# Program order on the DMA queue, later input requests, longer runs for v, and scaling ahead of the exponentials in a fused retention and mixture-of-attention kernel

## The chip, the cores and the metric

The kernel runs on one core of one Trainium2 chip. The metric is the device time of one execution in microseconds (us); lower is better. Engines are named as in the profile: PE is TensorE (PEld its weight loads), DVE is VectorE, ACT is ScalarE, POOL is GpSimd, SP is SyncE, which here only issues DMAs.

## The reference, cut to what matters

Eight batches, sequence S = 576. First a causal retention with decay over eight heads of width 64; its result x (576 x 512 per batch) goes into a second stage, a causal softmax attention for four experts, whose outputs are mixed with the weights of the two best experts of each token.

```
scores = (q @ k.T) / 8                       # per head, 576 x 576
x      = (scores * gamma**(i-j) * causal) @ v
logits = x @ w_gate;  w = softmax over the top 2 of 4 experts
for e in range(4):
    qe, ke, ve = x @ wq[e], x @ wk[e], x @ wv[e]
    a  = softmax(causal(qe @ ke.T / 8))
    out += w[e] * (a @ ve) @ wo[e]           # only where e is among the top 2
```

All is float32; the projections, v and the output product are done with operands split into a high and a low part (three products each).

## The kernel before, in words

**Tiles.** A batch is five chunks of tokens: four of 128 and one of 64 (CH, L20). The main loop (L532) runs n over 40 chunks of all batches and two more; in step n the retention works on chunk n and n-1, and the softmax attention on chunk n-6 (LAG, L26). Step n belongs to one of five kinds, n mod 5, because the heavier work of the second stage is dealt out by a table (STEPS, L448 to L461):

- kind 3: projections to q and k for tokens 0 to 255 (kq0);
- kind 4: projection to v for those tokens (v0, two tiles) and two output blocks (o0);
- kind 0: the two other output blocks of o0 and four of o1 (tokens 256 to 575), six in all;
- kind 1: half of the projections kq1 for tokens 256 to 575, and v1 (three tiles);
- kind 2: the other half of kq1, with the product of attention weights and v (`values`, L408) dealt between its pieces.

**One step** (L532 to L581) issues, in this order: `load(n + 2)` (two input DMAs, x and vk); `factors` (L374: three small DVE operations that make the row factors of the chunk whose exponentials ran one step earlier); `qk` (L127), the first part of `result` (L146: products `old` and `own`, ACT copies `old` out of PSUM at L168, DVE adds at L183), `state` (L106, product `st`); `scores(n - 6)` (L323: product `ss`; DVE masks each row block and takes its maximum, L361 or L365, tile nm; ACT takes the exponential in place with the row sum, L369); gate work; the rest of `result` (POOL multiplies at L188, and scales the next vk by L104; ACT rounds to xh at L191; POOL makes xl at L193); then the work of the table. Between the pieces of that work it deals `spread` (L402): one `scale` (L385: ACT multiplies a block of the exponentials by its row factor, L389) followed by one `turn` (L392: DVE transposes the block into TA and TB, L397 and L399). In a step of kind 2 the scales are dealt between the pieces, and the turns come after all of them, because `values` still reads TA and TB.

**PSUM** has eight banks, one pool (L42, L50). A product's bank comes free when ACT or DVE has copied it out: `pj` of a projection at L240 and L242, `pv` at L263, `po` of an output block at L442 (ACT) or L440 (DVE), `ys` of values at L424 and L425. The tile ot behind an output block has four buffers (L438), each free again when its output DMA (L443) has landed.

**v by way of HBM.** v is projected with tokens on partitions and needed in another arrangement, so it is written to HBM (tile hv, L267 and L268, one DMA) and read back with four DMAs (`back`, L274 to L279), one for each quarter of the partitions of vq. The runs that these four read are 512 bytes (128 floats). `back` is called behind the whole work of the step after the one that wrote hv (L574 to L578). vq for tokens 256 to 575 has one buffer, so its read waits until `values` of the batch before has read the old one.

**Order.** PE, DVE, ACT and POOL keep the order of the program (ORDERED, L15, `manual_schedule` at L43). SP isn't among them: the order of its DMAs is the compiler's, from its own planned times, and each waits in the queue for the one ahead.

**The tail** (L489) does the last five chunks of the last batch, with no retention beside it.

The functions that the diff touches, and what calls them:

Of the kernel before, what the change touches and what calls it, by code (L numbers as in the profile page):

```python
# [8 lines left out]
F32 = mybir.dt.float32  # L9
# [2 lines left out]
AF = mybir.ActivationFunctionType  # L12
OP = mybir.AluOpType
AX = mybir.AxisListType
ORDERED = {mybir.EngineType.PE, mybir.EngineType.DVE, mybir.EngineType.Activation, mybir.EngineType.Pool}  # L15

B, H, S, D = 8, 8, 576, 64
E, DM = 4, 512
# [5 lines left out]
NC = 5 * B  # L24

LAG = 6  # L26
# [7 lines left out]
def kernel(ctx: ExitStack, tc: tile.TileContext, xf, xt, vkf, vkt,  # L34
                                                    wraw, gi_d, con_d, out):
    nc = tc.nc
# [4 lines left out]
    hbm = ctx.enter_context(tc.tile_pool(name="hbm", bufs=2, space=bass.MemoryType.DRAM))  # L41
# [7 lines left out]
    def bank(shape, name):  # L49
        return pool.tile(shape, F32, name=name, tag="b")  # L50
# [31 lines left out]
    QUAD = [slice(32 * g, 32 * g + 32) for g in range(4)]  # L82
# [115 lines left out]
    W, QK, VN, WT = {}, {}, {}, {}  # L198
# [46 lines left out]
    def vproj(b, r, t):  # L245
        r0, n, tiles = RNG[r]
        nt = len(tiles)
        t0, C = CH[t]
        l0, ti = t0 - r0, t - tiles[0]
        xh, xl = XR[b, r]  # L250
        if ti == 0:
            VN[b, r] = (sb.tile([128, nt, NWV], F32, name=f"vn{r}", bufs=1),
                        sb.tile([128, 4 * nt, 2 * D], F32, name=f"vq{r}", bufs=2 - r))
        vn, vq = VN[b, r]
        ps = bank([128, NWV], "pv")
        i = 0
        for xx, ww in ((xh, W["v"][0]), (xh, W["v"][1]), (xl, W["v"][0])):
            for kc in range(4):
                mm(ps, xx[:, kc, l0:l0 + 128], ww[:, kc], start=(i == 0), stop=(i == 11))  # L259
                i += 1  # L260
                if i % 4 == 0 and i < 12:
                    yield
        act(vn[:, ti], ps, AF.Copy)  # L263
        if t == tiles[-1]:
            GATES.append(gate(b, r))

            hv = hbm.tile([128 * nt, E * D], F32, name=f"hv{r}")  # L267
            nc.sync.dma_start(hv.rearrange("(t p) c -> p t c", p=128), vn[:, :, :E * D])  # L268
            LATER.append((vq, hv))
        yield  # L270

    LATER = []

    def back():  # L274
        while LATER:
            vq, hv = LATER.pop()
            for g in range(4):
                p = g // 2
                nc.sync.dma_start(vq[QUAD[g]], hv[:, 128 * p:128 * p + 128].rearrange("(j r) c -> r j c", r=32))  # L279


    GATES = []
# [91 lines left out]
    def factors(m):  # L374
        b, t = divmod(m, 5)
        r = 0 if t < 2 else 1
        ti = t - RNG[r][2][0]
        p32, sm, ws = SS[m]
        n = len(ws)
        rs = sm[:, 1, :n]  # L380
        v.tensor_scalar(sm[:, 0, :n], sm[:, 0, :n], 1e-9, None, op0=OP.add)
        v.reciprocal(rs, sm[:, 0, :n])
        v.tensor_mul(rs, rs, WT[b, r][:, ti].rearrange("p i z -> p (i z)")[:, :n])  # L383

    def scale(m):  # L385
        p32, sm, ws = SS[m]
        for u, w in enumerate(ws):
            x = p32[:, u, :w]
            act(x, x, AF.Copy, scale=sm[:, 1, u:u + 1])  # L389
            yield  # L390

    def turn(m):  # L392
        p32, sm, ws = SS.pop(m)
        for u, w in enumerate(ws):
            z, k, nb = u % 2, 2 * (m % 5) + u // 2, w // 32
            x = p32[:, u, :w].rearrange("p (j c) -> p j c", c=32)
            v.transpose(TA[:, :min(nb, 8), z, k], x[:, :min(nb, 8)])  # L397
            if nb > 8:
                v.transpose(TB[:, :nb - 8, z, k - 4], x[:, 8:])  # L399
            yield  # L400

    def spread(m):  # L402
        a, b = scale(m), turn(m)
        for _ in a:
            next(b)
            yield

    def values(b, s0, s1):  # L408
        py = [bank([128, s1 - s0, 32], "ys") for g in range(4)]
        for j in range(2 * s1):  # L410
            sj = max(s0, j // 2)
            vq, jj = VN[b, 0 if j < 8 else 1][1], j % 8 if j < 8 else j - 8
            for z in range(2):
                tt = TA[:, j, z, sj:s1] if j < 8 else TB[:, j - 8, z, sj - 4:s1 - 4]
                for g in range(4):
                    mm(py[g][HALF[z], sj - s0:], vq[QUAD[g], jj, D * z:D * z + D], tt[QUAD[g]],  # L416
                       start=(j == 0), stop=(j == 2 * s1 - 1))
            if j % 6 == 5 and j < 2 * s1 - 1:
                yield
        if b not in YU:  # L420
            YU[b] = [sb.tile([128, 2, 9, 2, 32], F32R, name=x, bufs=1) for x in ("yh", "yl")]
        for g in range(4):
            hi, lo = (y[:, g // 2, s0:s1, g % 2] for y in YU[b])
            act(hi, py[g], AF.Copy)  # L424
            v.tensor_sub(lo, py[g], f(hi))  # L425
        yield
# [21 lines left out]
    STEPS = {}  # L448
# [14 lines left out]
    def work(n):  # L463
        vals = [values(b, 0, 9) for b, kind, part in STEPS.get(n, []) if kind == "y"]
        for b, kind, part in STEPS.get(n, []):
            if kind == "y":
                continue
            r, i = int(kind[-1]), 0
            if kind[:-1] == "kq":
                for p in range(2) if part is None else [part]:  # L470
                    for w in "kq":
                        for _ in proj(b, r, w, p):
                            i += 1
                            for y in vals[:i % 2 == 0]:
                                next(y, None)
                            yield
            elif kind[:-1] == "v":
                for t in RNG[r][2] if part is None else [part]:
                    yield from vproj(b, r, t)
            else:  # L480
                for d in part:
                    yield from outproj(b, r, d)

    def run(g):
        for _ in g:
            pass


    def tail():  # L489
        b = B - 1  # L490
        t0 = NC - 5

        def beside(g, *hs):
            for _ in g:
                for h in hs:
                    next(h, None)

        def outs(b, r):
            for d in range(4):
                yield from outproj(b, r, d)  # L500

        factors(t0)
        run(scores(t0 + 1))
        gates()
        beside(work(NC + 2), scale(t0))
        back()
        factors(t0 + 1)
        gates()
        run(scores(t0 + 2))
        run(scale(t0 + 1))  # L510
        run(turn(t0))
        run(turn(t0 + 1))
        factors(t0 + 2)
        run(scores(t0 + 3))
        beside(outs(b - 1, 0), spread(t0 + 2))
        run(scores(t0 + 4))
        factors(t0 + 3)
        beside(outs(b - 1, 1), spread(t0 + 3))
        run(values(b, 0, 4))
        factors(t0 + 4)  # L520
        beside(outs(b, 0), spread(t0 + 4))
        run(values(b, 4, 9))
        run(outs(b, 1))

# [5 lines left out]
    fetch("q")  # L530
    decay(0)
    for n in range(NC + 2):  # L532
        load(n + 2)
        if n == 1:
            nc.sync.dma_start(rg, wraw[:, 4096:].rearrange("p (k w) -> p k w", k=4))
            nc.sync.dma_start(mask[:, 448:], con_d[:, 92:])
        if n in (1, 4):
            fetch("v" if n == 1 else "o")
        late = result(n - 1) if 1 <= n <= NC else iter(())
        if n == LAG + 1:  # L540
            gates()
        if n > LAG:
            factors(n - LAG - 1)
        if n < 3:

            next(late, None)
            if n == 2:
                weights("k", "h")
            qk(n)
            next(late, None)  # L550
            state(n)
            run(late)
        else:
            if n < NC:
                qk(n)
            next(late, None)
            if n < NC:
                state(n)
        if n >= LAG:
            run(scores(n - LAG))  # L560
        gates()
        if n > 5:
            run(late)
        else:
            decay(n + 1)
        for w in {2: "kq", 3: "v", 6: "o"}.get(n, ""):
            weights(w, "l" if w == "k" else "hl")
        spreads, turns = iter(()), iter(())
        if n > LAG:
            if any(kind == "y" for _, kind, _ in STEPS.get(n, [])):  # L570
                spreads, turns = scale(n - LAG - 1), turn(n - LAG - 1)
            else:
                spreads = spread(n - LAG - 1)
        held = LATER[:]  # L574
        for _ in work(n):
            next(spreads, None)
        if held:
            back()  # L578
        run(spreads)
        run(turns)  # L580
        run(late)  # L581
    tail()
# [54 lines left out]
```

## Time and profile before

| | |
|---|---|
| median of 3 runs | 478.84 us (475.49 to 482.30) |
| profiled execution | 478.31 us |
| its span, first to last instruction | 476.6 us |
| mean granted clock of TensorE, as a share of full speed | 0.95 |
| DMA packets | 49245, of which 38400 under 2 KB (4096 of them under 512 B) |
| moved by the core's DMAs | 66.7 MB |

The span is 1.7 us shorter than the execution's own time, for what lies before the first and behind the last instruction. Busy time of an engine is the time in which it executes; idle time in brackets stands just ahead of an instruction and names what ended it, "issue" where the profile shows nothing that it waited for. The granted clock is a share of full speed: 1.00 is the upper level of TensorE's clock, 2.4 GHz, 0.50 the lower, 1.2 GHz.

### The profile page before, as it was taken

The page shows a single profiled execution, that of the slowest core. Times are in us where ns is not written, and L with a number is a line of the kernel's source. Part 1 is how long each engine was busy: PE and PEld are TensorE (multiplying, and loading weights), DVE is VectorE, ACT ScalarE, POOL GpSimd, SP SyncE. Part 2 cuts the span into 40 slices and gives each one's busy share as a digit, 9 for nine tenths or more (in the row PEclk, how much of TensorE's full clock was granted, in tenths as well). Part 3 has the DMA queues.
Part 4 walks back from the last instruction along what each step waited for, and adds up shares of the span by engine and source line. Part 5 has one row for each costly group of instructions (what it writes and reads, how often), then busy time and mean ns, then how long its engine had stood idle before and what let it go on. Part 6 is the DMA issues. An engine that isn't in the chain of part 4 may idle for free.

```text
span 476.6 us, 21304 instructions
## 1 busy us (share of the span) xinstructions
PE 425.6 (89%) x9068; PEld 370.0 (78%) x9068; DVE 288.0 (60%) x1179; ACT 284.8 (60%) x858; POOL 173.4 (36%) x198
## 2 busy tenths in 40 slices
PE   6587998798998989899997999989998999998876
PEld 3487986787887878798886988888877978886665
DVE  2643777854677365763876537783767637664750
ACT  2445577753866557654666457664667547763762
POOL 2428465433344434343453325444354424200000
PEclk9669999899998999989997999999998999999789
DMA  8827563723474262732647426652548420323121
GB/s 286 318 87 249 153 178 141 190 80 75 173 196 149 80 157 91 228 124 76 167 148 213 143 54 194 180 168 81 158 140 250 124 61 12 115 88 69 45 101 58
DMA packets 49245, 66.72 MB, mean 140 GB/s; under 512 B 4096, under 2 KB 38400, under 8 KB 49152
## 3 DMA queue, kind: packets, MB, share of 16 engines
q1 hardware_dynamic: 49152, 65.38, 45.0%
q8 instruction: 71, 1.16, 1.1%
q14 instruction: 22, 0.18, 0.1%
HBM read 50.68 MB, written 14.68 MB: 137 GB/s over the span
## 4 chain that ended last, share of the span: by engine, by line
PE 51%; ACT 23%; DVE 15%; issue 5%; DMA 4%; POOL 1%; SPq 1%; DVEq 0%; ACTq 0%; POOLq 0%
PE pj L235 19%; PE ys L416 10%; ACT p L369 7%; ACT p L389 7%; PE pv L259 7%; PE po L436 3%; PE ss L343 3%; PE st L117 3%; DVE p L365 2%; PE own L178 2%; DVE x L183 2%; DMA vk<-vkf 2%; ACT ot L442 2%; DMA ta<-wraw 2%; PE qk L137 2%
## 5 line engine op out<-in xcount | busy, mean ns | idle before, releaser
L369 ACT ACTIVATE p<-p,nm 128x64 f32<-128x64 f32 (+5 forms) x144 | 79.5, 553 | 87.4 <-DVE nm L361 61.8
L143 POOL TENSOR_SCALAR_AFFINE_SELECT p<-p 64x512 f32<-64x512 f32 (+1 forms) x80 | 49.6, 620 | 156.3 <-ACT p L140 153.7
L397 DVE STREAM_TRANSPOSE ta<-p 128x256 f32<-128x256 f32 (+2 forms) x144 | 53.4, 387 | 41.3 <-ACT p L389 40.0
L389 ACT ACTIVATE p<-p,sm 128x64 f32<-128x64 f32 (+5 forms) x144 | 73.8, 551 | 1.5 <-DVE sm L383 1.5
L183 DVE TENSOR_TENSOR x<-x,own 128x256 f32<-128x256 f32 (+1 forms) x80 | 26.2, 360 | 54.1 <-ACT x L168 47.4
L361 DVE CUSTOM_DVE_ANT_0 p<-ss,mask 128x128 f32<-128x128 f32 (+7 forms) x128 | 50.7, 450 | 2.3 <-PE ss L343 2.3
L188 POOL TENSOR_TENSOR x<-x,gi 128x512 f32<-128x512 f32 (+1 forms) x38 | 44.5, 1171 | 18.9 <-DVE x L183 16.6
L425 DVE TENSOR_TENSOR yl<-ys,yh 128x288 fp32r<-128x288 f32 (+2 forms) x36 | 12.7, 414 | 57.7 <-ACT yh L424 57.7
L343 PE MATMUL ss<-k,q 64*64 64x512 f32 (+7 forms) x512 | 43.2, 423 | 3.2 <-issue 1.4
L193 POOL TENSOR_TENSOR x1l<-x,x1h 128x512 fp32r<-128x512 f32 (+1 forms) x24 | 26.5, 1105 | 48.9 <-ACT x1h L191 48.9
L117 PE MATMUL st<-vk 64*64 64x64 f32 x1024 | 28.3, 235 | 16.3 <-issue 9.3
L178 PE MATMUL own<-p,vk 64*64 64x64 f32 x1152 | 31.6, 226 | 12.0 <-ACT ot L442 4.6
L117 PEld LDWEIGHTS st<-vk 64*64 64x64 f32 x1024 | 23.6, 144 | 18.9 <-issue 10.3
L178 PEld LDWEIGHTS own<-p,vk 64*64 64x64 f32 x1152 | 26.2, 138 | 14.5 <-issue 13.9
L436 PE MATMUL po<-yh,who 128*128 128x320 f32 (+1 forms) x128 | 30.2, 316 | 4.9 <-ACT yh L424 3.5
L104 POOL TENSOR_TENSOR vk<-vk,con 128x512 f32<-128x512 f32 (+1 forms) x34 | 32.6, 958 | 0.1
L416 PE MATMUL ys<-ta,vq 32*64 32x288 f32 (+8 forms) x1152 | 31.2, 347 | 0.0
L140 ACT ACTIVATE p<-qk 128x256 f32<-128x256 f32 (+1 forms) x80 | 24.6, 364 | 8.8 <-PE qk L137 8.8
L436 PEld LDWEIGHTS po<-yh,who 128*128 128x128 f32 x128 | 21.7, 199 | 10.1 <-ACT yh L424 3.9
L436 PE MATMUL po<-yl,who 128*128 128x320 f32 (+1 forms) x128 | 29.0, 308 | 0.0
L242 ACT ACTIVATE q<-pj 128x256 f32<-128x256 f32 (+1 forms) x32 | 12.9, 402 | 26.5 <-PE pj L235 26.4
L343 PEld LDWEIGHTS ss<-k,q 64*64 64x64 f32 x512 | 21.3, 144 | 9.5 <-issue 3.9
(105 smaller groups left out, 1013.8 us busy)
## 6 DMA issues: line engine op xcount, KB each, us to landing
x<-xf SPq DMA_DIRECT2D x32, 512.0 KB, 4.6
vk<-vkf SPq DMA_DIRECT2D x32, 512.0 KB, 5.7
vq<-hv SPq DMA_DIRECT2D x32, 192.0 KB, 4.2
out<-ot SPq DMA_DIRECT2D x32, 160.0 KB, 2.6
vq<-hv SPq DMA_DIRECT2D x32, 128.0 KB, 4.8
out<-ot SPq DMA_DIRECT2D x32, 128.0 KB, 3.4
hv<-vn SPq DMA_DIRECT2D x8, 384.0 KB, 2.8
ta<-wraw SPq DMA_DIRECT2D x4, 512.0 KB, 8.5
```

The costliest lines, as they stand in the source:

```text
L117: mm(ps[r][HALF[g], s, u], vk[HALF[r], s, 1, h], vk[HALF[r], s, 0, h], start=True, stop=True)
L143: gp.affine_select(w, w, pattern=[[0, 4 * k], [1, 64]], base=0, channel_multiplier=-1, compare_op=OP.is_ge, fill=0.0)
L178: mm(own[r][HALF[u], g, i], vk[HALF[r], s, 0, 2 * g + u], p[HALF[r], g, s, u], start=True, stop=True)
L188: e.tensor_mul(x32, x32, gi[:, :, t0:t0 + C])
L235: mm(ps, ww[:, kc, p * 128:(p + 1) * 128], xx[:, kc, :n], start=(i == 0), stop=(i == 11))
L343: mm(ps[u][HALF[p]], q[p][HALF[z], l0 + 64 * i:l0 + 64 * i + 64], k[p][HALF[z], :ws[u]], start=True, stop=True)
L361: v.tensor_tensor_reduce(x, ps[u], mask[:, 512 - ws[u]:], -1.0, BIG, OP.add, OP.min, nm[:, u:u + 1])
L369: act(x, x, AF.Exp, bias=bias, scale=-1.0, accum_out=sm[:, 0, u:u + 1])
L389: act(x, x, AF.Copy, scale=sm[:, 1, u:u + 1])
L397: v.transpose(TA[:, :min(nb, 8), z, k], x[:, :min(nb, 8)])
L416: mm(py[g][HALF[z], sj - s0:], vq[QUAD[g], jj, D * z:D * z + D], tt[QUAD[g]], start=(j == 0), stop=(j == 2 * s1 - 1))
L436: mm(ps, ww[:, p, d * 128:(d + 1) * 128], yy[:, p], start=(i == 0), stop=(i == 5))
```

## The change

SP joins the engines that keep the program's order. From step 6 on `load(n + 2)` is issued behind the scores of the step instead of at its start. hv is written by two DMAs, one for each pair of experts, in an arrangement in which `back` reads runs of 1024 bytes (tokens 0 to 255) or 1536 bytes (the rest); vq's order of blocks changes with it (`jj` in `values`). `back` is called behind the third piece of the step's work. `scale` of a chunk runs as a whole behind the score products of the next chunk and ahead of that chunk's exponentials; only `turn` is still dealt between the pieces, or behind them in a step of kind 2. `values` issues its parts behind the first, third and fifth piece instead of the second, fourth and sixth. The tail is put in the same order.

```diff
-ORDERED = {PE, DVE, Activation, Pool}
+ORDERED = {PE, DVE, Activation, Pool, SP}
...
@@ vproj
-            hv = hbm.tile([128 * nt, E * D], F32, name=f"hv{r}")
-            nc.sync.dma_start(hv.rearrange("(t p) c -> p t c", p=128), vn[:, :, :E * D])
+            hv = hbm.tile([2, 128, nt * 2 * D], F32, name=f"hv{r}")
+            for p in range(2):
+                nc.sync.dma_start(hv[p].rearrange("q (t c) -> q t c", t=nt), vn[:, :, 2 * D * p:2 * D * p + 2 * D])
@@ back
             for g in range(4):
-                p = g // 2
-                nc.sync.dma_start(vq[QUAD[g]], hv[:, 128 * p:128 * p + 128].rearrange("(j r) c -> r j c", r=32))
+                nc.sync.dma_start(vq[QUAD[g]].rearrange("r (j t) c -> r j (t c)", j=4),
+                                  hv[g // 2].rearrange("(j r) x -> r j x", j=4))
...
-    def spread(m):
-        a, b = scale(m), turn(m)
-        for _ in a:
-            next(b)
-            yield
-
@@ values
-            vq, jj = VN[b, 0 if j < 8 else 1][1], j % 8 if j < 8 else j - 8
+            vq, i = VN[b, 0 if j < 8 else 1][1], j % 8 if j < 8 else j - 8
+            jj = i % 4 * (2 if j < 8 else 3) + i // 4
@@ work
-                            for y in vals[:i % 2 == 0]:
+                            for y in vals[:i % 2]:
@@ tail
+        def ahead(m):
+            soft = scores(m)
+            run(scale(m - 1))
+            run(soft)
+
         factors(t0)
-        run(scores(t0 + 1))
+        ahead(t0 + 1)
         gates()
-        beside(work(NC + 2), scale(t0))
+        run(work(NC + 2))
         back()
         factors(t0 + 1)
         gates()
-        run(scores(t0 + 2))
-        run(scale(t0 + 1))
+        ahead(t0 + 2)
         run(turn(t0))
         run(turn(t0 + 1))
         factors(t0 + 2)
-        run(scores(t0 + 3))
-        beside(outs(b - 1, 0), spread(t0 + 2))
-        run(scores(t0 + 4))
+        ahead(t0 + 3)
+        beside(outs(b - 1, 0), turn(t0 + 2))
         factors(t0 + 3)
-        beside(outs(b - 1, 1), spread(t0 + 3))
+        ahead(t0 + 4)
+        beside(outs(b - 1, 1), turn(t0 + 3))
         run(values(b, 0, 4))
         factors(t0 + 4)
-        beside(outs(b, 0), spread(t0 + 4))
+        beside(outs(b, 0), scale(t0 + 4), turn(t0 + 4))
@@ main loop
-        load(n + 2)
+        if n < LAG:
+            load(n + 2)
...
         if n >= LAG:
-            run(scores(n - LAG))
+            soft = scores(n - LAG)
+            if n > LAG:
+                run(scale(n - LAG - 1))
+            run(soft)
+            load(n + 2)
...
-        spreads, turns = iter(()), iter(())
-        if n > LAG:
-            if any(kind == "y" for _, kind, _ in STEPS.get(n, [])):
-                spreads, turns = scale(n - LAG - 1), turn(n - LAG - 1)
-            else:
-                spreads = spread(n - LAG - 1)
-        held = LATER[:]
-        for _ in work(n):
-            next(spreads, None)
-        if held:
-            back()
-        run(spreads)
+        turns, held = turn(n - LAG - 1) if n > LAG else iter(()), LATER[:]
+        hold = any(kind == "y" for _, kind, _ in STEPS.get(n, []))
+        for i, _ in enumerate(work(n)):
+            if not hold:
+                next(turns, None)
+            if i == 2 and held:
+                back()
         run(turns)
         run(late)
```

## Rows read from the trace of the kernel before

**Rows 1.** The page's busy time of each engine over the span.
```profile
PE 425.6 (89%) x9068; PEld 370.0 (78%) x9068; DVE 288.0 (60%) x1179; ACT 284.8 (60%) x858; POOL 173.4 (36%) x198
```

**Rows 2.** Busy time by stretch (start:end length; engines; granted clock; DMA share; GB/s).
```profile
72.00:96.00 24.00, 19.66 (x332) 16.65 (x332) 19.50 (x80) 17.49 (x54) 13.09 (x15) 0.93 0.54 162
...
216.00:240.00 24.00, 23.98 (x611) 20.17 (x610) 14.79 (x65) 14.68 (x49) 10.31 (x12) 1.00 0.46 127
240.00:264.00 24.00, 20.03 (x321) 18.31 (x320) 16.68 (x70) 16.52 (x49) 10.58 (x12) 0.86 0.58 184
...
348.00:372.00 24.00, 22.02 (x347) 19.75 (x340) 18.73 (x78) 17.95 (x52) 12.25 (x13) 0.93 0.70 212
...
432.00:477.00 45.00, 33.24 (x685) 27.22 (x671) 22.53 (x88) 21.82 (x59) 0.00 (x0) 0.89 0.25 72
```

**Rows 3.** PE in order of time, 244 to 259 us (start, length, operation, idle before).
```profile
244.69 0.45 PE L178 MATMUL own<-p,vk 64*64 64x64 f32 x12 [0.56 <-ACT vn L263]
...
254.38 0.68 PE L178 MATMUL own<-p,vk 64*64 64x64 f32 x28 [0.60 <-ACT ot L442]
257.51 1.29 PE L117 MATMUL st<-vk 64*64 64x64 f32 x30 [2.45 <-issue]
```

**Rows 4.** ACT in order of time, 235 to 258 us.
```profile
238.73 0.67 ACT L369 ACTIVATE p<-p,nm 128x448 f32<-128x448 f32 x1 [1.42 <-DVE nm L361]
...
241.99 1.00 ACT L389 ACTIVATE p<-p,sm 128x320 f32<-128x320 f32 x2
...
244.18 0.37 ACT L263 ACTIVATE vn<-pv 128x260 f32<-128x260 f32 x1
...
248.80 0.78 ACT L369 ACTIVATE p<-p,nm 128x576 f32<-128x576 f32 x1 [3.40 <-DVE nm L365]
...
251.49 0.66 ACT L389 ACTIVATE p<-p,sm 128x448 f32<-128x448 f32 x1
...
254.12 0.73 ACT L389 ACTIVATE p<-p,sm 128x512 f32<-128x512 f32 x1
256.98 0.77 ACT L442 ACTIVATE ot<-po 128x320 f32<-128x320 f32 x2 [2.13 <-DMA out<-ot]
```

**Rows 5.** The page's costliest groups: busy, mean ns, idle just before and its releaser.
```profile
L369 ACT ACTIVATE p<-p,nm 128x64 f32<-128x64 f32 (+5 forms) x144 | 79.5, 553 | 87.4 <-DVE nm L361 61.8
...
L389 ACT ACTIVATE p<-p,sm 128x64 f32<-128x64 f32 (+5 forms) x144 | 73.8, 551 | 1.5 <-DVE sm L383 1.5
```

**Rows 6.** DVE in order of time: the last of the factors, step of kind 0.
```profile
246.08 0.46 DVE L383 TENSOR_TENSOR sm<-sm,wt 128x4 f32<-128x4 f32 x1
```

**Rows 7.** DMA issues in 244 to 262 us, then in 411 to 420 us: KB, landing.
```profile
out<-ot SPq DMA_DIRECT2D x4, 128.0 KB, 4.3
...
out<-ot SPq DMA_DIRECT2D x2, 128.0 KB, 1.7
```

**Rows 8.** Busy time by stretch: inputs alone on the queue, then vq alone.
```profile
262.00:264.00 2.00, 2.00 (x10) 2.00 (x10) 1.89 (x6) 2.00 (x4) 1.40 (x2) 0.61 0.97 379
437.00:438.00 1.00, 1.00 (x12) 0.19 (x6) 0.84 (x6) 0.00 (x0) 0.00 (x0) 1.00 1.24 207
```

**Rows 9.** The start in order of time: SP, then DVE, then PE.
```profile
10.17 1.05 SPq L208 DMA_DIRECT2D ta<-wraw  x2
...
13.43 0.33 SPq L95 DMA_DIRECT2D vk<-vkf  x1
...
22.59 1.68 DVE L104 TENSOR_TENSOR vk<-vk,con 128x512 f32<-128x512 f32 x1 [1.22 <-DMA vk<-vkf]
...
25.46 1.22 PE L235 MATMUL pj<-xh,wlk 128*128 128x256 f32 x4 [2.81 <-DVE wlk L221]
```

**Rows 10.** PE in order of time, start of a step of kind 3.
```profile
283.88 0.39 PE L165 MATMUL old<-x,s 64*64 64x64 f32 x10 [0.64 <-issue]
```

**Rows 11.** PE in order of time in the tail.
```profile
444.86 3.00 PE L350 MATMUL ss<-k,q 64*64 64x288 f32 x16 [2.27 <-DVE nm L361]
...
457.85 0.92 PE L436 MATMUL po<-yh,who 128*128 128x256 f32 x2 [2.96 <-ACT yh L424]
```

More of the change, by code (lines that the diff above doesn't have):

```diff
@@ L14 @@
 AX = mybir.AxisListType
-ORDERED = {mybir.EngineType.PE, mybir.EngineType.DVE, mybir.EngineType.Activation, mybir.EngineType.Pool}
+ORDERED = {mybir.EngineType.PE, mybir.EngineType.DVE, mybir.EngineType.Activation, mybir.EngineType.Pool,
+           mybir.EngineType.SP}
 B, H, S, D = 8, 8, 576, 64
```

## The prediction, made before the changed kernel was run

> **What bounds the kernel now.** I read the page's busy times first. PE executes for 425.6 of 476.6 us; no other engine comes near [rows 1]. So what a change of order can win lies in PE's 51 us of idle time and in the time that PE runs at its lower clock. Then the stretches, to see where these are. Between 216 and 240 us PE is full (23.98 of 24). In the next 24 us it has 20.03, and the granted clock is 0.86 [rows 2]. The reader is to see that the loss isn't spread out: it returns once a batch, six times from 72 to 372 us. Read off those six stretches (the first, the third last and the last stand in [rows 2]; the others are 132 to 156, 180 to 216 and 300 to 324), the idle time is 4.34, 3.18, 2.66, 3.97, 2.64 and 1.98 us, 18.8 in all. The clock falls with it: the shares of full speed that are missing, times the lengths (0.14 x 24 = 3.4 us for the worked one), add up to 10.2 us. At most 84% of that counts, for PE was busy so long there (20.03 of 24): 8.5 us.
>
> PE in order of time shows which steps these are [rows 3]. At the start of a step of kind 0 it waits 0.56 us for vn (L263). At the start of a step of kind 1 it waits 0.60 us for an ot (L442), then 2.45 us in front of `st`, until 257.51. "Issue" stands there, but ACT's last two ot end at 257.75 and the first of them near 257.4, and that frees the bank [rows 4]. So PE waits for PSUM banks, that ACT empties too late. ACT's order shows why: it stood idle 1.42 and 3.40 us ahead of the exponentials, waiting for DVE's maxima, and put the four scales (0.66 to 0.73 us each in kind 0) between the copies that PE waits for [rows 4]. Over the run that idle is 87.4 us, and all scales are 73.8 us [rows 5].
>
> **The change part by part.** The sum is made against the profiled execution, 478.3 us, which lies 0.1% from the median of the runs, 478.84.
>
> *Scales ahead of the exponentials.* Nothing is added; 144 ACT operations move. Kind 4: two pairs, 1.00 us the first and an estimated 1.1 the wider second, fill the idle 1.42, so the exponentials come 0.7 us later. But the second vn (now done at 244.55) no longer has 2.1 us of scales ahead of it: 244.55 - 2.1 + 0.7 = 243.15, which is 1.4 earlier, more than PE's wait of 0.56 [rows 3, 4]. Kind 0: DVE's factors end at 246.54 [rows 6]. They stand behind transposes that themselves waited for scales, so they move about 1 us forward, to 245.5. Four scales, 2.8 us, end at 248.3. The maxima are ready a microsecond earlier too (247.8 for 248.80), so the exponentials start 0.5 us later than they could, at 248.3. From their start to the end of the first ot ACT takes 2.7 us (248.80 to the scale at 251.49 [rows 4]): 251.0; five more at 0.39 (0.77 for two) end at 252.9, if nothing holds them.
>
> *What is late next.* The fifth ot needs a buffer, so the landing of the output sent first, at about 251.0. Under the inputs that took 4.3 us in this stretch, on a quieter queue 1.7 [rows 7]; before, the fifth waited 2.13 us for it [rows 4]. In program order the two inputs of 512 KB go out at about 245 and are through before 250 (1.05 MB at 379 GB/s is 2.8 us [rows 8]), and vq's reads come behind the third output. So I take a landing near the quiet one, 2.2: the last two ot end near 254.0 (251.0 + 2.2 + 0.77) and `st` starts near 254.1, 3.4 us earlier, of the 3.97 lost in that stretch. I let 0.9 us stay per batch (0.6 here, more where an output lands later). Sum: 18.8 - 6 x 0.9 = **13.4 us**. Bounds: with the loaded landing of 4.3, the end is 2.1 us later and 13.4 - 6 x 1.2 = 6.2 us are left; with none, 18.8. If half of the slow clock goes with the gaps, **4 us** of the 8.5; bounds 0 and 8.5.
>
> *Program order at the start.* Now SP sends the weights for v and o (10.17) ahead of vk of chunk 3 (13.43) [rows 9]. In program order vk comes first, because o is fetched in step 4 and v behind `load(3)`. That takes 1.09 MB out of its way, 2.9 us at 379 GB/s [rows 8]. But DVE was idle only 1.22 us for it, and PE's 2.81 us hang behind on that operation and on the low part of wk [rows 9]. **1.2 us**; bounds 0 (x of chunk 3 waits for its buffer) and 2.8. v's weights come later by those two inputs; they are rounded only at the end of step 3, behind the projections of step 2, and that covers it.
>
> *Inputs behind the scores.* Two DMAs per step start later by what `qk` to `ss` take; what they bring is first read most of a step later, by POOL (L104), behind its masks and L188. Nothing: the step's own work covers it. Were the cover gone, POOL would wait at L104 with the mask of the next `p` behind it, and `own` on PE behind that. Bounds -2 (that wait, once or twice) and 0.
>
> *hv in two writes, v back in longer runs, mid-step.* 16 DMA issues are added, at 0.33 to 0.5 us each [rows 9], on a queue that isn't on the path; 64 reads carry half or a third of the runs. The back read for tokens 256 to 575 still waits for `values` and stands at the head of SP meanwhile; behind it stands only the next step's input. The trace shows vq's 512-byte runs alone at 207 GB/s with the queue's share at 1.24, inputs in longer runs at 379 with 0.97 [rows 8]: runs of 512 bytes go slower here. So a read of 512 KB shrinks from 2.5 us towards 1.4. Nobody waits for vq, so I count 0; bounds 0 and 1.1 us in each of six batches, 6.6, should it free the outputs' way.
>
> The Trainium skill (DMA: Bandwidth & Descriptors, Specifications) says that 512 bytes is the smallest transfer that reaches line rate; by it the longer runs give nothing and that upper end is 0. The row with 207 beside 379 speaks against it.
>
> *`values` a piece earlier.* Five times PE pauses at the start of kind 3, behind the last part of `values`, 0.64 us in the row shown [rows 10]; a projection piece now lies between that part and the next step, so that its four banks empty under cover. The cause named is only "issue", so **1 us** of 5 x 0.64 = 3.2; bounds 0 and 3.2.
>
> *The tail.* 11.8 us of 45 are idle [rows 2], the largest pieces 2.27 behind DVE's maxima and 2.96 behind the copies of `values` [rows 11]. DVE stood behind transposes that waited for scales; these now come sooner. Against it, factors of the last chunk but one now stand ahead of the last maxima and wait for exponentials. **1.5 us**; bounds -2 and 5.
>
> Sum: 13.4 + 4 + 1.2 + 1 + 1.5 = 21.1; 478.3 - 21.1 = 457.2, **457 us**.
>
> **The rivals.**
>
> *A. The wait changes hands.* The ot buffers decide: outputs land as slowly as now (4.3 us), ACT stands at the fifth ot, and the clock still falls. Then 6.2 + 1.2 + 1 = 8.4 us are won: 470 us. For it: the 2.13 us at the fifth ot are already there [rows 4]. Against: the inputs leave the outputs' way.
>
> *B. Slower: the first copy of a step instead of the last.* Scales that don't fit the idle time push exponentials, xh and with them the first copy out of PSUM: 0.7 us in kind 4, as much in kinds 0 and 3. If PE's bank is freed by that first copy, the push is paid in three steps of seven batches: 0.7 x 21 = 14.7 us, less 1.2 at the start: 492 us. It decides from the point at which the factors (246.54) end less than four scales, 2.8 us, ahead of the maxima (248.80): that is so already by 0.5 us. Against it: PE's waits name the second vn and a later ot, not the first copies [rows 3].
>
> *C. Given back.* PE is full from 216 to 240 us, kinds 2 to 4 [rows 2]; if such steps are in truth paced by DVE and ACT, PE arrives earlier and waits there. Then only the start and pieces are won: 476 us. Against: ACT and DVE work 15 of 24 us there.
>
> *D. All of it.* PE's busy time itself may be stretched. Weight loads take 370.0 us [rows 1]; in the full stretch they are 20.17 of 24 [rows 2]. At that rate the whole takes 370.0 x 24 / 20.17 = 440 us. The Trainium skill (Perfetto Trace Analysis, Identifying the Most-Contended Engine) says that matmul busy time misjudges how much is left and that the share of weight loads is the better measure; going by that rule, 440. No row tells that this order reaches it.
>
> **How the numbers follow.** Forecast, 447 to 466: 0.62. A, 466 to 473: 0.18. C, 473 to 480: 0.09. B, 485 to 495: 0.07. D: 0.04. A measurement of this kernel tells about 2% from no change, so faster begins at 469: the forecast, D and half of A, 0.75. Same: the other half of A and C, 0.18. Slower: B, 0.07. The low end: 457 less the untaken rest of the boundaries (5.4) and of the clock (4.5) is 447; 446. The high end covers A: 471.
>
> **What would show it right or wrong.** Right: ACT's idle ahead of L369 falls from 87 us below 40; DVE no longer waits for scales; the stretch with kinds 4 and 0 holds PE above 22.5 of 24; the clock stays at 1.00 in most of them; a batch takes some 3 us less. Rival A: a wait of ACT's ot for an output of over 1.5 us in each batch. B: PE waiting for the first vn or ot. C: new idle time of PE in kinds 1 to 3. Wrong altogether: POOL waiting at L104 for vk, or SP standing in front of inputs.

## The result: 439.85 us, and where the 38 us went

| | before | after |
|---|---|---|
| median of 4 runs | 478.17 us (475.49 to 482.30) | 439.85 us (439.00 to 445.25) |
| span of the profiled execution | 476.6 us | 437.0 us |
| mean granted clock | 0.950 | 0.977 |

The ratio is 0.9215, with a 95% interval of 0.9114 to 0.9317. Ratios here and below are taken from runs within 1.5% of the fastest of their kernel: for e3 that leaves two of four, 455.97 and 462.62 us, and its trace is of its slowest, 463.65 us. The forecast was 457 us with a range of 446 to 471: the direction was right, the gain nearly twice what was forecast.

The page of the changed kernel gives the busy times, against [rows 1].

```profile
span 437.0 us, 21343 instructions
...
PE 408.2 (93%) x9068; PEld 355.6 (81%) x9068; DVE 285.4 (65%) x1179; ACT 286.2 (65%) x858; POOL 173.3 (40%) x198
```

PE's idle time has gone from 51.0 to 28.8 us. Its busy time fell too, by 17.4 us, with the same 9068 products; the two make up the 39.6 us by which the span is shorter. The greater part of those 17.4 us is the clock: its missing share over the span was 0.050 x 476.6 = 23.8 us and is 0.023 x 437.0 = 10.1 us, 13.7 less. At least 3.7 us of busy time went for another reason, to which the account of the prediction comes back.

The stretches of [rows 2] begin and end in the middle of steps. So I read the same work on both sides, from the start of `qk` in a step of kind 0 to its start in kind 2 (columns as in [rows 2]). Two of six batches, and in the third line the tail, from the last `qk` to the end; first before, then after:

```profile
243.10:269.36 26.26, 22.29 (x337) 20.57 (x336) 17.74 (x74) 14.68 (x43) 9.02 (x11) 0.87 0.50 158
...
299.81:322.08 22.27, 19.63 (x337) 18.08 (x336) 17.69 (x73) 14.38 (x43) 8.96 (x11) 1.00 0.65 184
...
399.64:476.60 76.96, 65.39 (x1181) 54.58 (x1180) 41.59 (x177) 44.00 (x126) 4.87 (x6) 0.93 0.24 74
```
```profile
222.20:241.34 19.14, 18.52 (x338) 17.31 (x337) 15.26 (x66) 13.31 (x39) 9.35 (x11) 1.00 0.68 216
...
271.89:291.24 19.35, 18.54 (x338) 17.29 (x337) 15.24 (x66) 13.38 (x39) 9.35 (x11) 1.00 0.66 212
...
365.44:437.00 71.56, 63.23 (x1181) 52.69 (x1180) 40.25 (x175) 43.90 (x126) 4.87 (x6) 0.98 0.26 79
```

The steps of kinds 0 and 1 took 22 to 26 us and take 18 to 19. PE lacks 0.4 to 0.8 us in them instead of 2.0 to 4.2, and the clock is 1.00 in all six batches. In the tail 8.3 us are idle instead of 11.6, and the clock is 0.98 instead of 0.93.

The page's groups of the exponentials (L371 now) and of the scales (L391), against [rows 5]:

```profile
L371 ACT ACTIVATE p<-p,nm 128x64 f32<-128x64 f32 (+5 forms) x144 | 79.3, 553 | 14.3 <-DVE nm L363 12.5
L391 ACT ACTIVATE p<-p,sm 128x64 f32<-128x64 f32 (+5 forms) x144 | 69.8, 565 | 10.0 <-DVE sm L385 9.0
```

ACT's idle time ahead of the exponentials is 14.3 us instead of 87.4. Some of it now stands ahead of the scales, which wait for DVE's factors: 10.0 instead of 1.5.

ACT in order of time in a step of kind 0, against [rows 4]:

```profile
223.79 2.47 ACT L391 ACTIVATE p<-p,sm 128x448 f32<-128x448 f32 x4
...
226.38 0.78 ACT L371 ACTIVATE p<-p,nm 128x576 f32<-128x576 f32 x1
...
228.81 1.29 ACT L439 ACTIVATE ot<-po 128x256 f32<-128x256 f32 x4
...
231.45 0.77 ACT L439 ACTIVATE ot<-po 128x320 f32<-128x320 f32 x2 [1.34 <-PE own L179]
```

Four scales run without a gap, then the exponentials, then four copies in one piece. The wait of 1.34 us that is left is ahead of the fifth: it is named after PE, but a fifth ot needs a buffer, and with more buffers the wait goes (below). PE in the same step and behind it, in kind 1, against [rows 3]:

```profile
223.18 0.68 PE L118 MATMUL st<-vk 64*64 64x64 f32 x32
...
229.93 0.69 PE L138 MATMUL qk<-x 64*64 64x64 f32 x32
...
231.98 0.90 PE L118 MATMUL st<-vk 64*64 64x64 f32 x30 [0.62 <-issue]
```

The pause ahead of `st` in kind 1 is 0.62 us instead of 2.45, and PE goes through 30 products of `st` in 0.90 us instead of 1.29. Without any pause ahead of them, in the step of kind 0, 32 take 0.68.

Step by step (from the start of one step's `qk` on PE to that of the next, mean of the last five batches) the kernels that matter stand so, in us:

| kernel | kind 3 | kind 4 | kind 0 | kind 1 | kind 2 |
|---|---|---|---|---|---|
| before | 10.70 | 7.48 | 8.96 | 14.97 | 12.85 |
| after | 10.18 | 7.47 | 7.72 | 11.42 | 13.23 |
| e1_scale_back | 10.18 | 7.48 | 9.10 | 12.74 | 13.33 |
| e2_scale_only | 10.58 | 7.48 | 7.72 | 15.93 | 12.87 |
| e3_sp_free | 10.11 | 7.47 | 7.72 | 16.17 | 13.17 |
| e4_ot5 | 10.73 | 7.47 | 8.95 | 14.23 | 12.94 |
| f1_scale_and_order | 10.53 | 7.48 | 7.72 | 11.29 | 13.00 |
| g1_scale_and_buffers | 10.46 | 7.47 | 7.72 | 10.17 | 12.96 |
| g2_after_buffers | 10.11 | 7.47 | 7.72 | 10.16 | 13.34 |
| g3_before_buffers | 10.61 | 7.48 | 9.04 | 12.75 | 12.86 |

Over the whole span kind 1 gives 21.3 us and kind 0 gives 7.7, together 29.0 of the 39.6. All behind the last `qk` (step 39), the tail for the most part, gives 5.4 (77.0 to 71.6), the first step of kind 4 with work of the second stage (step 9) 1.8, the steps ahead of it 1.7, kinds 2 and 3 together 1.7. In the last five batches kind 2 gives back what kind 3 gains, but for 0.1 us in each: the earlier parts of `values` move a boundary and little else.

### The profile page after: what moved, and what is told of

It reads as the page before. It is cut to its first block, busy times and chain, and to the rows that moved or that the text cites. A ratio compares the mean times of both kernels' runs of the same rounds, so it can differ in the third digit from the quotient of the medians.

```text
span 437.0 us, 21343 instructions
## 1 busy us (share of the span) xinstructions
PE 408.2 (93%) x9068; PEld 355.6 (81%) x9068; DVE 285.4 (65%) x1179; ACT 286.2 (65%) x858; POOL 173.3 (40%) x198
## 4 chain that ended last, share of the span: by engine, by line
PE 81%; DVE 6%; ACT 4%; issue 3%; DMA 3%; SPq 1%; POOL 1%; ACTq 0%; DVEq 0%; POOLq 0%
PE pj L236 25%; PE pv L260 12%; PE ys L413 11%; PE po L433 10%; PE ss L345 8%; PE qk L138 4%; PE st L118 4%; PE own L179 3%; PE old L166 3%; DMA vk<-vkf 3%; PE ss L352 2%; DVE p L363 1%; DVE wlk L222 1%; DVE ta L399 1%; ACT ot L439 1%
## 5 line engine op out<-in xcount | busy, mean ns | idle before, releaser
L371 ACT ACTIVATE p<-p,nm 128x64 f32<-128x64 f32 (+5 forms) x144 | 79.3, 553 | 14.3 <-DVE nm L363 12.5
L391 ACT ACTIVATE p<-p,sm 128x64 f32<-128x64 f32 (+5 forms) x144 | 69.8, 565 | 10.0 <-DVE sm L385 9.0
L399 DVE STREAM_TRANSPOSE ta<-p 128x256 f32<-128x256 f32 (+2 forms) x144 | 49.4, 368 | 0.4
L345 PE MATMUL ss<-k,q 64*64 64x448 f32 (+7 forms) x512 | 41.4, 409 | 2.1 <-ACT p L141 1.0
L141 ACT ACTIVATE p<-qk 128x256 f32<-128x256 f32 (+1 forms) x80 | 24.8, 367 | 13.7 <-PE qk L138 13.7
L421 ACT ACTIVATE yh<-ys 128x288 fp32r<-128x288 f32 (+2 forms) x36 | 10.9, 391 | 34.3 <-PE ys L413 34.3
L118 PE MATMUL st<-vk 64*64 64x64 f32 x1024 | 25.0, 226 | 6.9 <-issue 4.1
L179 PE MATMUL own<-p,vk 64*64 64x64 f32 x1152 | 27.5, 225 | 3.9 <-issue 3.9
L264 ACT ACTIVATE vn<-pv 128x260 f32<-128x260 f32 x40 | 14.6, 383 | 21.9 <-PE pv L260 21.8
L118 PEld LDWEIGHTS st<-vk 64*64 64x64 f32 x1024 | 21.2, 139 | 8.9 <-issue 5.1
L413 PEld LDWEIGHTS ys<-ta,vq 32*64 32x64 f32 x1152 | 23.1, 131 | 6.2 <-issue 3.4
L433 PE MATMUL po<-yh,wlo 128*128 128x320 f32 (+1 forms) x128 | 27.9, 300 | 0.0
```

The source lines that it names most:

```text
L118: mm(ps[r][HALF[g], s, u], vk[HALF[r], s, 1, h], vk[HALF[r], s, 0, h], start=True, stop=True)
L345: mm(ps[u][HALF[p]], q[p][HALF[z], l0 + 64 * i:l0 + 64 * i + 64], k[p][HALF[z], :ws[u]], start=True, stop=True)
L371: act(x, x, AF.Exp, bias=bias, scale=-1.0, accum_out=sm[:, 0, u:u + 1])
L433: mm(ps, ww[:, p, d * 128:(d + 1) * 128], yy[:, p], start=(i == 0), stop=(i == 5))
```

## The experiments

Three theories stood against each other. S: the move of the scales carries the gain. Q: the program's order of DMA issues carries it, because the outputs land sooner. P, formed after the first four runs: neither alone, the two together.

### One part taken back, one part alone

**e1_scale_back**: the changed kernel with the scales dealt between the pieces again, in the loop and in the tail.

```diff
-            soft = scores(n - LAG)
-            if n > LAG:
-                run(scale(n - LAG - 1))
-            run(soft)
+            run(scores(n - LAG))
...
+            next(spreads, None)
```

> The changed kernel with one part undone: scales dealt between the pieces of a step's work again, each ahead of its transpose, in the loop and in the tail; queue order, longer runs and the rest stay. Theory S (the place of the scales is nearly the whole gain: ACT empties PSUM too late, PE waits for banks, and the lower clock follows): 465 to 473 us, PE idle again at the starts of kinds 0 and 1, granted clock back near 0.95. Theory Q (the DMA queue's order is the gain: outputs land sooner, so ACT isn't held at the fifth ot): 443 to 452 us.

Measured 466.32 us, ratio 0.9771 (0.9718 to 0.9824). Two of the waits in its trace (engine, tile and line, what ended the wait: us in total, times, longest):

```profile
ACT p L371 <- DVE nm L363: 61.2, 32, 3.2
...
PE own L179 <- ACT ot L445: 4.2, 8, 0.6
```

The idle time ahead of the exponentials and PE's wait for an ot are back as before (61.2 and 4.2 us, before 61.8 and 4.6), and kind 0 is back at 9.10. Everything else of the change, without the scales, is worth 2.3% (1.8 to 2.8) of the 7.9.

**e2_scale_only**: the kernel before, with the scales ahead in loop and tail and nothing else.

```diff
-            run(scores(n - LAG))
+            soft = scores(n - LAG)
+            if n > LAG:
+                run(scale(n - LAG - 1))
+            run(soft)
...
```

> The kernel before with one part alone: scales ahead of the next exponentials, in the loop and in the tail; SP unordered, inputs at the step's start, 512-byte runs, back at the step's end, values dealt as before. Theory S: 443 to 452 us. Theory Q: 462 to 472 us.

Measured 461.43 us, ratio 0.9656 (0.9605 to 0.9707): far from S's number and just under Q's. Kind 0 is as fast as in the changed kernel, 7.72, but kind 1 is slower than before, 15.93. ACT in order of time shows why:

```profile
234.45 2.47 ACT L389 ACTIVATE p<-p,sm 128x448 f32<-128x448 f32 x4
...
239.46 1.29 ACT L442 ACTIVATE ot<-po 128x256 f32<-128x256 f32 x4
245.51 0.77 ACT L442 ACTIVATE ot<-po 128x320 f32<-128x320 f32 x2 [4.76 <-DMA out<-ot]
```

The four copies come together, as planned, and the fifth stands for 4.76 us, until an output has landed. PE then waits 4.04 us ahead of `st`. The queue in order of time (SP), and the landing of the outputs in 236 to 248 us (KB, us from issue to landing):

```profile
237.43 0.35 SPq L91 DMA_DIRECT2D x<-xf  x1
237.89 0.36 SPq L95 DMA_DIRECT2D vk<-vkf  x1
238.31 1.05 SPq L279 DMA_DIRECT2D vq<-hv  x2
239.85 6.93 SPq L443 DMA_DIRECT2D out<-ot  x6
```
```profile
out<-ot SPq DMA_DIRECT2D x2, 128.0 KB, 5.5
```

By the compiler's order the first output goes out at 239.85, behind two inputs that left only 2 us before and two of vq's reads, and takes 5.5 us. In the changed kernel the same stretch is this, with the landing of the two outputs of 128 KB sent from 229.20 on:

```profile
226.09 0.38 SPq L92 DMA_DIRECT2D x<-xf  x1
226.57 0.39 SPq L96 DMA_DIRECT2D vk<-vkf  x1
229.20 1.30 SPq L440 DMA_DIRECT2D out<-ot  x3
230.55 1.88 SPq L280 DMA_DIRECT2D vq<-hv  x4
232.53 2.64 SPq L440 DMA_DIRECT2D out<-ot  x3
```
```profile
out<-ot SPq DMA_DIRECT2D x2, 128.0 KB, 2.1
```

The inputs have 2.6 us of lead, three outputs go ahead of vq's reads, and the landing takes 2.1 us. So with the scales alone the wait of rival A is what happens, with a landing of 5.5 us where I had priced it with 4.3.

**e3_sp_free**: the changed kernel, with SP in the compiler's order.

```diff
-ORDERED = {PE, DVE, Activation, Pool, SP}
+ORDERED = {PE, DVE, Activation, Pool}
```

> The changed kernel with SP taken out of the engines that keep the program's order. Theory S: 438 to 445 us, within 1% of the changed kernel, the start 1 us later. Theory Q: 452 to 465 us, with ACT held at an ot for an output in every batch.

Measured 463.01 us (455.97 to 463.65), ratio 0.9624 (0.9508 to 0.9739). The waits of this trace, and under them the same two of the changed kernel's:

```profile
ACT ot L438 <- DMA out<-ot: 25.0, 7, 5.5
...
PE st L117 <- issue: 20.9, 7, 4.8
```
```profile
ACT ot L439 <- DMA out<-ot: 6.0, 5, 1.5
...
PE st L118 <- issue: 4.1, 7, 0.9
```

Without the order the fifth copy waits seven times for 25.0 us in all, instead of five times for 6.0, and PE waits behind it. e2, in the compiler's order too, has the same waits: 21.7 us, seven times. This hits Q's number, as e1 and e4 hit S's: each half seems necessary, which is what P says.

**e4_ot5**: the kernel before, with five buffers for ot.

```diff
-        ot = sb.tile([128, n], F32, name="ot", tag="ot", bufs=4)
+        ot = sb.tile([128, n], F32, name="ot", tag="ot", bufs=5)
```

> The kernel before with five buffers for ot instead of four, so that the fifth copy of a batch no longer waits for the landing of the third. Theory S: 472 to 479 us, ACT's wait for outputs (5.0 us before) nearly gone and little won. Theory Q: 455 to 468 us.

Measured 474.25 us, ratio 0.9969 (0.9930 to 1.0008): S's number. But the wait that e4 was to take away hardly went, against 5.0 us before:

```profile
ACT ot L442 <- DMA out<-ot: 3.7, 5, 1.8
```

In the step looked at it is now the sixth copy that waits, 1.80 us. So e4 doesn't tell S from Q; g3 below, with six buffers, takes the greater part of the wait away.

### The pair, and the small parts

**f1_scale_and_order**: e2 with SP in the program's order, and nothing else of the change.

```diff
-ORDERED = {PE, DVE, Activation, Pool}
+ORDERED = {PE, DVE, Activation, Pool, SP}
```

> The kernel before with two parts of the change: scales ahead of the next exponentials, and SP in program order; inputs still at the step's start, 512-byte runs, back behind the whole work, values dealt as before. Theory P (the two are a pair: scales ahead bring the six copies together, and the fifth waits for the third's output to land; program order puts the outputs ahead of vq and behind inputs that are already through): 440 to 446 us, ACT's wait for outputs below 8 us in all against 21.7 with the scales alone. Theory R (it is the other edits on the queue, the place of the inputs or the longer runs, that let outputs land): 453 to 462 us, wait still near 20 us.

Measured 438.89 us, ratio 0.9187 (0.9095 to 0.9279). That is a little under P's number, and within these intervals the two edits are the whole change. The wait for outputs is 5.2 us in its trace:

```profile
ACT ot L443 <- DMA out<-ot: 5.2, 6, 1.0
```

The runs also show that the two don't just add: e2 alone gives 0.0344 of the time and the other parts without the scales (e1) 0.0229, together 0.0573, while the pair gives 0.0813.

**e6_load_start**, **e7_short_runs** and **e10_back_end** each take one small part out of the changed kernel: inputs asked for at the start of the step; hv in one write and read in 512-byte runs, as before; vq's reads behind the whole work of the step.

```diff
-        if n < LAG:
-            load(n + 2)
+        load(n + 2)
...
-            load(n + 2)
```

> The changed kernel with the inputs asked for at the step's start again. Theory P: 438 to 442 us, nothing lost. Theory R: 450 to 460 us, because the inputs meet the outputs.

```diff
-            hv = hbm.tile([2, 128, nt * 2 * D], F32, name=f"hv{r}")
+            hv = hbm.tile([128 * nt, E * D], F32, name=f"hv{r}")
...
```

> The changed kernel with hv in one write and vq read in 512-byte runs again. Theory P: 438 to 443 us; the outputs behind vq's reads land later, but nothing waits for those. Theory R: 446 to 456 us.

```diff
-            if i == 2 and held:
-                back()
+        if held:
+            back()
```

> The changed kernel with v read back behind the whole work of the step again, so all six outputs of kind 0 stand ahead of vq's reads. Theory P: 437 to 442 us, the fifth copy waits for the same landing as before or a little less. If the place in mid-step matters by itself: 445 us or more.

Measured 438.51 (ratio 0.9200, 0.9143 to 0.9257), 438.91 (0.9203, 0.9130 to 0.9276) and 437.99 us (0.9190, 0.9130 to 0.9251), beside 438.89 for f1. None of the three can be told from the changed kernel, and f1, which lacks all of them and the edit to `values` too, can't either. So I call each of them nothing, within the half of a per cent to a whole one that these intervals leave.

### Another way to the same end: more buffers

**g1_scale_and_buffers**: e2 (SP in the compiler's order) with six buffers for ot, two for tokens 0 to 255 and four for the rest. To make room, two small constant tiles share the space of others. **g2_after_buffers** and **g3_before_buffers** put the same into the changed kernel and into the kernel before.

```diff
-        ot = sb.tile([128, n], F32, name="ot", tag="ot", bufs=4)
+        ot = sb.tile([128, n], F32, name="ot", tag=f"ot{r}", bufs=4 if r else 2)
...
-    wz = const.tile([128, 128], BF16, name="wz")
-    v.memset(wz, 0.0)
+    wz = mask[:, :64].bitcast(BF16)
...
-    rg = const.tile([128, 4, E], F32, name="rg")
+    rg = TB.rearrange("p j z s c -> p (j z s c)")[:, :4 * E].rearrange("p (k e) -> p k e", k=4)
```

> The kernel before with scales ahead of the next exponentials and more room for outputs instead of the new queue order: ot has two buffers for tokens 0 to 255 and four for the rest, so no copy waits for an output of its own batch (room made by laying the zeros of the warm-up and the raw gate weights into other tiles). SP unordered. If the queue order helps only through the landing that the fifth copy waits for (theory P): 438 to 446 us, ACT's wait for outputs under 3 us. If the order acts otherwise as well (transfers slowing engines, inputs late): 450 to 460 us with that wait gone.

> The changed kernel with the same six buffers for ot: ACT's 6.0 us of waits for outputs and PE's pauses of 0.5 to 0.8 us ahead of st in kind 1 go. Theory P: 434 to 438 us. A gain over 8 us would say that more hung on this wait than the rows show.

> The kernel before with these six buffers for ot alone. Theory P: 464 to 473 us, the same as the queue order without the scales (466.3), because both take the wait for the landing away and leave ACT's scales between the copies. If buffers do nothing by themselves: 474 to 479 us.

Measured: g1 434.28 us (ratio 0.9099, 0.9045 to 0.9152), g2 431.64 (0.9046, 0.8996 to 0.9097), g3 469.38 (0.9815, 0.9739 to 0.9891). g3 came out as P said, g1 and g2 below P's numbers. ACT waits for no output in g1 and once, 1.0 us, in g2; kind 1 takes 10.17 and 10.16 us. The waits ahead of `st`, 9.3 us before and 4.1 in the changed kernel, are these, g1 first:

```profile
PE st L116 <- issue: 2.2, 3, 1.4
```
```profile
PE st L117 <- issue: 1.4, 2, 1.1
```

In g3 ACT's idle time ahead of the exponentials and PE's wait for an ot stay where they were:

```profile
ACT p L368 <- DVE nm L360: 61.5, 32, 3.2
...
PE own L177 <- ACT ot L441: 4.6, 8, 0.6
```

But in the step where PE waited 2.45 us ahead of `st` it waits 0.21 in g3, as in e1, and kind 1 takes 12.75 us as in e1 (12.74). So that pause was the wait for the landing; what the scales cost in kind 1 is the rest, from 12.75 to g1's 10.17.

The wait for the landing can be made short by the order of the queue or be taken away by buffers. With the buffers the compiler's order costs little: g1's four runs (432.92 to 434.92 us) lie above g2's (431.14 to 432.01), 0.6% between the medians, and g2 has the small parts too. The buffers alone give 1.9% (1.1 to 2.6), on top of the scales 9.0 - 3.4 = 5.6% of the time before. This takes the place of the label "PE own" that the profile put on ACT's wait: the wait was for the buffer. g2 is faster than both kernels. Its gain over the changed kernel, 8.2 us between the medians and 7.0 between the spans of the traces, stands at the 8 us above which, by its expectation, more hung on this wait than the rows show; the account of the prediction says what.

### The tail

**e8_tail_back**: the changed kernel with the tail of the kernel before.

```diff
-        ahead(t0 + 1)
+        run(scores(t0 + 1))
...
-        beside(outs(b - 1, 0), turn(t0 + 2))
+        beside(outs(b - 1, 0), spread(t0 + 2))
...
```

> The changed kernel with the tail in the order of the kernel before, the loop as changed. If the tail's order is worth what the traces differ by from the last step of kind 4 on (5.4 us): 444 to 446 us. If that difference came from the loop's last steps, and the tail is worth the 1.5 us of the prediction: 439 to 442 us.

Measured 447.42 us, ratio 0.9392 (0.9323 to 0.9462), above both numbers. In its trace 87.25 us follow the start of `qk` in step 38, in the changed kernel's 82.33: 4.9 us. The medians are 7.6 us apart; the other part lies in the loop, where the code is the same, and is not settled. PE in order of time in the tail, first with the old tail, then in the changed kernel, against [rows 11]:

```profile
411.50 3.00 PE L352 MATMUL ss<-k,q 64*64 64x288 f32 x16 [2.10 <-DVE nm L363]
...
424.48 0.72 PE L439 MATMUL po<-yh,who 128*128 128x256 f32 x2 [3.11 <-ACT yh L427]
```
```profile
407.34 2.48 PE L352 MATMUL ss<-k,q 64*64 64x288 f32 x16 [0.91 <-DVE nm L363]
...
417.93 0.72 PE L433 MATMUL po<-yh,who 128*128 128x256 f32 x2 [1.84 <-ACT yh L421]
```

Both pauses are shorter by more than a microsecond, and the score products run in 2.48 us instead of 3.00.

## Why the prediction was right in kind and wrong in size

**The slow clock, 4 us: the term that failed.** Taken for kinds 4, 0 and 1 were 13.4 us of idle time and 4 us of clock, 17.4; kinds 0 and 1 gave 29.0, more than the upper bounds of the two terms together (18.8 + 8.5 = 27.3). Read over the six batches from the `qk` of kind 0 to that of kind 2, PE's idle time went from 18.7 to 3.7 us and its busy time from 123.7 to 109.6. So the idle term was about right, 14.9 for 13.4, and the 0.9 us that I let stay per batch are 0.6. The other term is the step that failed, "If half of the slow clock goes with the gaps, 4 us of the 8.5": PE's busy time in these steps fell by 14.1 us, over three times the term and more than its upper bound.

Three things were wrong in it. The first is "At most 84% of that counts, for PE was busy so long there". The clock is not low evenly over such a stretch: where it fell, PE then worked without a gap at the lower level. The trace of before shows it just behind the pause that ended at 257.51:

```profile
258.00:260.00 2.00, 2.00 (x46) 1.67 (x43) 1.33 (x7) 0.64 (x4) 1.48 (x3) 0.50 0.47 162
260.00:262.00 2.00, 2.00 (x9) 2.00 (x8) 1.93 (x12) 1.68 (x9) 2.00 (x2) 0.50 0.48 135
```

PE is busy 2.00 of 2.00 us at a clock of 0.50. Of the 3.4 us missing in that stretch, 2 us fall into these 4 us and 0.8 into the next two, which run full at 0.61 [rows 8]: little is to be cut off. (Not every batch had this: from 299.81 to 322.08 the clock stayed at 1.00 with 2.6 us of pauses.) The second is the half. All of the missing clock, some 10.2 us, went: behind the pauses that are left, 0.62 us in the stretch shown, the clock is 1.00 throughout.

The third is that some 3.9 of the 14.1 us are more than the clock can give, and the prediction has no term for them. In the batch from 299.81 on the clock was 1.00 before and is 1.00 after, and PE's busy time still fell from 19.63 to 18.54 us. A pause costs more than its length even so. Here is the step of kind 1 with the pause of 0.62 us, in the changed kernel, and the same step in g2, where the pause is gone:

```profile
229.93:241.34 11.41, 10.79 (x190) 10.29 (x189) 8.82 (x37) 6.70 (x22) 4.89 (x5) 1.00 0.74 231
```
```profile
227.43:237.56 10.13, 10.13 (x189) 9.82 (x188) 8.80 (x37) 6.65 (x22) 4.90 (x5) 1.00 0.79 256
```

The step is 1.28 us shorter for a pause of 0.62, at a clock of 1.00 in both. Part of the rest lies in the products just behind the pause: 30 of `st` take 0.90 us there, 32 take 0.68 without it. Why they are slow is not shown.

**The mechanism held.** The fifth ot did become what is late next, by 1.34 us, and `st` waits 0.62 us behind it, where I had worked out 0.6. One reading of before was off: I put the 2.45 us ahead of `st` down to the scales between the copies, and with these in place g3 and e1 leave 0.21 of it; it was the landing. That a landing near the quiet one (2.2 assumed, 2.1 measured for those outputs) needs the queue's order is shown by e2 and e3. The wait of rival A is thus true of the scales alone: there the fifth copy waited 4.8 us, and kind 1 came out at 15.93 instead of 14.97. My price for A was too high all the same: 470 us, and e2 took 461.43, since kind 0 keeps its gain there, and so does all behind the last `qk` (71.5 us). Its sum was wrong besides: it counts 1.2 us a batch where the landing just put in makes 0.9 + 2.1 = 3.0, which would have given 475.

**The tail, 1.5 us, gave about 5.** From the last `qk` on it is 5.4 us by the traces, 4.9 by e8's; its bound was 5. PE's idle time fell by 3.2 us there; the two pauses that I had counted, 2.27 and 2.96 us, lost 1.36 and 1.12 of it. Its busy time fell by 2.2 us, and the clock rose from 0.93 to 0.98: this I had left out.

**`values` a piece earlier, 1 us, gave next to nothing.** Kinds 2 and 3 together take 23.41 us instead of 23.55, and 23.53 in f1, which lacks the edit: 0.1 us a batch, which the runs can't tell from none. The pauses at the start of kind 3 are still there (0.49 us at 255.98, in the step of [rows 10]), so the cover that I counted on did not come.

**The start, 1.2 us: not there, and not shown elsewhere.** vk of chunk 3 does come sooner, and DVE doesn't wait for it any more. But DVE's next operation, which runs beside a subtraction of the same shape on POOL, takes 3.37 us and ends at 25.31, and PE starts its product at 25.36 instead of 25.46 [rows 9]. DVE in order of time, then POOL, then PE:

```profile
21.34 0.68 DVE L105 TENSOR_TENSOR vk<-vk,con 128x512 f32<-128x512 f32 x1
21.94 3.37 DVE L222 TENSOR_TENSOR wlk<-ta,whk 128x1024 fp32r<-128x1024 f32 x1
```
```profile
21.77 2.45 POOL L222 TENSOR_TENSOR wlq<-ta,whq 128x1024 fp32r<-128x1024 f32 x1 [1.23 <-issue]
```
```profile
25.36 1.22 PE L236 MATMUL pj<-xh,wlk 128*128 128x256 f32 x4 [2.55 <-DVE wlk L222]
```

`qk` of step 4 starts only 0.1 us earlier than before. The lead grows behind it, to 1.0 us by step 5 and 1.7 by step 9, but one execution can't put that down to the order: e2, in the compiler's order, is at step 9 at 66.44 us, the changed kernel at 67.50, the kernel before at 69.19.

**Inputs behind the scores, longer runs, vq's reads in mid-step: nothing**, as predicted, and e6, e7 and e10 show it one by one. There my reading of [rows 8] was wrong, too. It set vq's 512-byte runs, 207 GB/s, beside inputs at 379 and took the run length for the cause. In the tail vq's four reads of 192 KB go alone on the queue: they land in 3.9 us in 512-byte runs (e7) and in 3.7 in runs of 1536, and move 198 GB/s (402.0 to 403.5 us) and 214 (401.0 to 402.5). So a longer run is worth some 8% of the speed here, not the step from 2.5 us to 1.4 that I wrote, and what makes inputs faster is not shown. Nobody waited for vq anyway.

**The other rivals.** B (the first copies become late) and C (the time is given back) did not come: kind 4 takes 7.47 us as before, kind 0 less, and kinds 2 and 3 lose nothing together. D, 440 us, is what was measured, though I gave it 0.04. That is luck, for its sum doesn't hold: weight loads take 355.6 us now, not the 370.0 that I had put in; with 355.6 the same working gives 423 us; and g2 is faster still. The Trainium skill (Perfetto Trace Analysis, Identifying the Most-Contended Engine) takes the share of weight loads, beside that of peak arithmetic, as a better measure of what is left than matmul busy time. The trace agrees that busy time, 425.6 us, was no floor, but neither was the time of the weight loads.

## What to carry to other kernels

In these traces a gap in front of PE cost its own length, the slow clock behind it where the clock fell, and slower products just behind it: 14.9 us of gaps went, and 29.0 us with them. Count all three, the tail's too, where the profile shows the granted clock low just behind the gaps and PE full. An operation that the bottleneck doesn't wait for, put between copies out of PSUM, can make PE wait; let it run in the idle time ahead of them. Then ask what else the copies need: copies that come in a bunch need enough staging buffers (six copies, six buffers here), or a queue in which the first output isn't behind large reads.

## What the runs showed that I had not expected

- The clock can fall with a single pause. In e2 PE waits 4.04 us ahead of `st`, and over 246 to 250 us, where it is busy for 3.96 of 4, the granted clock is 0.57 (below). That step of kind 1 takes 16.25 us, the same step in g1 10.13: 6.1 us for a wait of 4.

```profile
246.00:250.00 4.00, 3.96 (x56) 3.57 (x57) 2.73 (x18) 3.62 (x14) 2.95 (x4) 0.57 0.72 231
```

- At the start, whichever DVE operation runs beside POOL's wlq is the long one: before, the product vk with 1.68 us [rows 9], where it takes 0.68 now, and now wlk's subtraction with 3.37 us, where it took 1.21. That the two engines disturb each other was not tried by itself.
- An output of 128 KB takes 5.5 us behind two inputs of 512 KB that were sent 2 us before, and 2.1 us when they have 2.6 us of lead and vq's reads come after.
- Reads of vq in 512-byte runs or in long ones give the same time of the kernel: 438.91 (e7) beside 439.85 us.
